# The first FFN layer of the last 512 tokens as seven block products, and a new order of steps

## The chip, the cores and the metric

The kernel runs on one NeuronCore of a Trainium2 chip. The core has engines that each work through a queue of their own in order: TensorE (PE, matrix products, with its weight loads shown apart as PEld), VectorE (DVE), ScalarE (ACT), GpSimd (POOL) and SyncE (SP, which only issues transfers). They wait for one another through semaphores. Products are written to PSUM, which PE, DVE and ACT reach and POOL does not; everything else lies in SBUF. The metric is the device time of one execution in microseconds (us).

## The reference

Windowed attention over 4 sequences of 768 tokens, 8 heads of 64, followed by a feed-forward network on all 3072 tokens with 512 features. A query sees the first 8 keys and the last 96 keys up to its own, with a bias that falls with distance.

```python
scores = scale * np.matmul(q, k.transpose(0, 1, 3, 2)) + bias     # per batch and head
scores = np.where(keep, scores, -1e9)                             # 8 global keys, 96 local ones
a = softmax(scores)
x = np.matmul(a, v).transpose(0, 2, 1, 3).reshape(3072, 512)
h = x @ w_in                                                      # 512 -> 2048
g = np.maximum(h, 0.0) + np.log1p(np.exp(-np.abs(h)))             # softplus
out = g @ w_out                                                   # 2048 -> 512, float32
```

## The kernel before

The 3072 tokens are 24 blocks of 128 for attention (index n, six to a sequence) and 12 chunks of 256 for the feed-forward network (index c, so chunk c takes blocks 2c and 2c+1). Everything is issued by one list of step names, `ORDER` (L564 on), written out in the file: the loop at its end calls one small function for each name, and each engine's queue gets its instructions in that order. Nothing is reordered later. The pools of tiles decide which step has to wait for which buffer.

The steps that matter here, with their names in the list:

- `lq`, `lk`, `lv`, `wi`, `wo`: loads, issued by POOL, which also turns float32 to 16 bits on the way (L101, L107, L112).
- `t`, `d`, `qc`, `kc`, `s`, `ss`, `ab`, `ac`, `e`, `p`, `nm`: transposes, scores, bias, exponential, product with v and normalisation of an attention block. `gk`, `gv` (L254, L259) copy the 8 global rows of k and v into the neighbouring block's tile.
- `x`, `xc`, `y`: the attention output transposed into `XT[c]`, bf16, 512 features by 256 tokens.
- `f` (`ffn1`, L410): the first layer, 8 steps a chunk, each two blocks of 128 hidden features: 8 matmuls of 256 columns into one bank `hT`, of which there are two.
- `fe`, `fl` (`soft`, `plus`): exponential by ACT out of `hT`, then ln(1 + x) by ACT into `G[c]`, float16.
- `o`, `os`: the second layer of chunk 0 in the plain way.
- `m` (`prod`, L499), `ev` (`evict`, L524), `pr` (`pair`, L549), `gs` (`g_sum`, L474), `wd`: the second layer of chunks 1 to 11 as seven block products after Strassen and Winograd: sums of blocks of G by DVE, differences of w_out blocks made once, each product evicted by DVE, two of the sums by POOL.
- `st`: stores, issued by SP. `g` (`gate`, L559): a one-element copy on POOL that makes the loads behind it wait for a step of ACT.

The functions of these steps follow; the seven products of `m` are listed as `BLOCKS`, and `ffn1` in the same place has the plain product.

Of the kernel before, what the change touches and what calls it, by code (L numbers as in the profile page):

```python
# [20 lines left out]
def kernel(  # L21
# [279 lines left out]
    def sc(n, half):  # L301

        if n < NPB:
            buf = early(n, half)
            qk(n, half, lambda r: buf[:, r, :], pre=True)
            return
        qk(n, half, lambda r: s_ps[:, r, :])

# [8 lines left out]
    def add_bias(n, half):  # L317

        Z = new_Z(n, half)
        if n == first_of(n):  # L320
            nc.vector.tensor_tensor(Z[:, 0:4, :], s_ps[:, 0:8:2, :], bias0[:, half, :, :], ALU.add)
        else:
            nc.vector.tensor_tensor(Z[:], s_ps[:], biasA[:, half, :, :], ALU.add)  # L323

    def add_bias2(n, i):

# [9 lines left out]
    def ex(n, half):  # L336
        nreg = 4 if n == first_of(n) else 8
        Pb = work4.tile([P, 8, P], BF16, tag="Pb", name="Pb")
        if n < NPB:
# [86 lines left out]
    def plus(c, u):  # L426
        if c not in G:
            G[c] = ffn.tile([P, NFB, CT], F16, tag="G", name="G")
        nc.scalar.activation(  # L429
            G[c][:, 2 * u : 2 * u + 2, :], ES.pop((c, u))[:], AF.Ln, bias=1.0  # L430
        )

    def o_bank(i):
# [125 lines left out]
    def gate(s):  # L559
# [3 lines left out]

    ORDER = """  # L564
        w18 bb1.0 cq0 ck0 bb0.0 lq1 tq0 lk1 tk0 lv0 z0.0 lk2 z0.1 s0.0 bb0.1 e0.0 lq2 bb1.1 t1 qc1.0
        kc1.0 lv1 s0.1 e0.1 lk3 lq3 z1.0 s1.0 e1.0 p0.0 nm0.0 z1.1 s1.1 t2 qc2.0 kc2.0 lv2 lv3 z2.0
        wi0 e1.1 wi1 p0.1 nm0.1 gk2 p1.0 nm1.0 p1.1 nm1.1 gv2 s2.0 z2.1 wi2 lq4 e2.0 s2.1 e2.1 t3
        qc3.0 kc3.0 gk3 x0 xc0.1 z3.0 p2.0 nm2.0 p2.1 nm2.1 s3.0 x1 xc1.0 e3.0 z3.1 lk4 gv3 s3.1 x2
        xc2.0 e3.1 p3.0 nm3.0 f0 fe0 fl0 lq5 p3.1 nm3.1 f1 fe1 fl1 wi3 x3 xc3.0 f2 fe2 f10 fe10 fl2
        gk4 gv4 fl10 t4 f9 fe9 qc4.0 f8 kc4.0 s4.0 f11 lk5 ab4.0 fe8 t5 qc5.0 fl9 fl8 wi4 fe11 fl11  # L570
        kc5.0 s4.1 ab4.1 e4.0 f3 fe3 fl3 f4 fe4 e4.1 gk5 s5.0 lv4 p4.0 fl4 ab5.0 f5 f12 s5.1 nm4.0
        p4.1 gv5 fe12 e5.0 fe5 fl5 fl12 wo0 o0 f13 nm4.1 x4 wi6 fe13 fl13 o4 f15 fe15 f14 lv5 wo1
        ab5.1 e5.1 p5.0 nm5.0 f6 wd1.0 wd1.1 fe6 p5.1 fl6 nm5.1 xc4.0 o1 o5 wo2 x5 xc5.0 gs1.3 fl15
        wo3 lq6 g11 fe14 fl14 g15 f7 wd3.0 fe7 o6 o2 f17 lk6 fl7 o7 f21 t6 gs1.1 gs1.2 fe21 qc6.1
# [24 lines left out]
        m5.5.0 ev5.5 nm16.0 fl54 ss17 ab17.0 ac17.1 fe51 fl51 d18 ac17.0 f52 p16.1 nm16.1 pr4.1 g47
        fe52 f59 g39 m4.3.0 gk18 lk19 g43 f56 ss18 lq19 fl52 lv17 fe59 e17.0 gv17 fe56 p17.0 e17.1  # L600
        ev4.3 nm17.0 g41 f58 lq20 lk20 ab18.0 f57 fl56 p17.1 fl59 ac18.1 fe58 fe57 fl57 gs6.3 nm17.1
        lv18 st3.1 e18.0 m5.2.0 st3.0 ac18.0 m6.1.1 f61 p18.0 ev5.2 f62 fe62 gs6.1 m6.5.0 gs6.2
        gs5.4 d19 fl58 ev6.1 fe61 fl61 ev6.5 ss19 gk20 ab19.0 f63 m7.1.0 e18.1 f60 fe63 ac19.1 y16
        lv20 ev7.1 nm18.0 ac19.0 y17 m6.6.1 p18.1 d20 pr5.0 m5.4.0 ev6.6 nm18.1 m5.3.1 g57 gs7.3
        ev5.3 e19.0 lv19 p19.0 nm19.0 f69 fl62 fe60 f64 e19.1 lk21 fl60 fl63 gs7.1 p19.1 gs7.2 gk19
        fe69 fl69 y18 ss20 f65 nm19.1 lq21 d21 y19 ev5.4 ab20.0 gk21 fe64 fe65 fl64 gv20 e20.0 f70
        m6.7.0 fe70 ac20.1 fl65 f71 fe71 lk22 p20.0 m7.5.1 ac20.0 e20.1 lq22 d22 fl71 f66 fe66 ev6.7
        pr5.1 ev7.5 pr6.0 m7.6.0 gs6.4 nm20.0 ss21 ab21.0 ev7.6 fl66 p20.1 f68 fe68 lv21 f67 fl68
        e21.0 ac21.1 gv21 nm20.1 m6.2.0 ac21.0 m6.4.1 fe67 e21.1 g53 p21.0 lk23 lq23 st4.1 g51 fl70
        f72 st4.0 ev6.4 ev6.2 g61 f75 nm21.0 g55 lv22 y20 pr7.0 p21.1 pr6.1 fe72 gk22 ss22 nm21.1  # L610
        fl67 ab22.0 m7.7.0 gv22 ev7.7 ac22.1 ac22.0 g49 g67 fl72 fe75 e22.0 f74 f77 m6.3.0 g65
        m8.1.1 d23 y21 p22.0 st5.1 fe77 fl75 e22.1 fl77 fe74 gv12 fl74 ev6.3 gk23 lv23 gs7.4 ev8.1
        f78 m7.2.0 nm22.0 gs8.1 p22.1 g59 st5.0 ev7.2 gv23 ss23 ab23.0 ac23.1 ac23.0 fe78 fl78 f76
        fe76 f73 e23.0 g63 fe73 m7.4.0 m8.5.1 fl73 nm22.1 p23.0 e23.1 f80 fe80 fl76 f85 nm23.0 p23.1
        fe85 fl85 ev7.4 ev8.5 gs9.3 pr7.1 m9.1.0 y22 st6.0 gs8.2 ev9.1 f87 f79 fl80 fe87 m7.3.1
        nm23.1 fe79 fl79 fl87 gs9.1 ev7.3 f84 fe84 f83 m8.6.0 m9.5.1 gs9.2 ev8.6 fl84 gs8.4 fe83 f82
        m8.2.0 st6.1 fe82 fl82 f86 fe86 fl86 f81 ev8.2 g69 fe81 fl81 gs8.3 pr8.0 m8.7.0 ev9.5 ev8.7
        y23 st7.0 m9.2.1 fl83 f93 m9.6.0 st7.1 ev9.2 f88 ev9.6 m8.4.1 ev8.4 m8.3.0 ev8.3 pr8.1 gv19
        fe88 fe93 fl93 fl88 f90 g73 fe90 m10.1.1 ev10.1 f95 fe95 fl90 fl95 gv18 f91 m9.7.0 f89
        gs10.1 gs10.2 gs10.4 m10.6.1 ev10.6 pr9.0 fe91 gs10.3 ev9.7 fe89 f92 f94 m10.7.1 gs9.4 fl91  # L620
        fl89 ev10.7 gs11.3 m10.5.0 fe94 ev10.5 st8.0 st8.1 m10.4.1 ev10.4 pr10.1 fl94 fe92 st10.1
        fl92 gs11.1 m9.4.0 ev9.4 pr9.1 m9.3.1 ev9.3 gs11.2 st9.0 st9.1 m11.1.0 ev11.1 m11.5.1 ev11.5
        m11.6.0 ev11.6 pr10.0 m11.7.1 ev11.7 m11.4.0 ev11.4 pr11.1 m10.2.1 pr11.0 st11.1 ev10.2
        gs11.4 m10.3.0 ev10.3 m11.2.1 st10.0 m11.3.2.1 ev11.2 ev11.3.1 st11.0.1 m11.3.2.0 ev11.3.0
        gv13 st11.0.0
    """

    def warm(count):
# [74 lines left out]
```

## Time and profile before

| | |
|---|---|
| median of 3 runs | 208.21 us (206.58 to 208.42) |
| the profiled execution | 207.14 us, span 205.3 us from the first to the last instruction |
| PE busy | 198.9 us, 97% of the span |
| ACT busy | 154.8 us, 75% |
| DVE busy | 151.0 us, 74% |
| POOL busy | 94.2 us, 46% |
| granted TensorE clock | 0.998 of full speed |

Busy times are of the profiled execution. A row of the timeline gives the start, the time until the group's end, engine, line, operation, the tiles written and read, and the count; square brackets hold the idle time before it and what ended that. A row of a group gives busy time and the mean of one, then the idle time before. A row of the stretches gives the busy time of each engine in a part of the span, with the number of instructions in parentheses.

### The profile page before, as it was taken

How to read it: one execution, taken by the hardware profiler on the slowest of the kernel's cores; microseconds unless marked ns; L12 is line 12 of the kernel's file. 1: busy time of each engine (PE TensorE's matmuls, PEld its weight loads, DVE VectorE, ACT ScalarE, POOL GpSimd, SP SyncE). 2: the span in 40 equal slices, each digit the busy share in tenths (PEclk: the TensorE clock that was granted, in tenths of full speed). 3: DMA queues.
4: the chain of work that ended last, by engine and by line, in shares of the span. 5: the costliest groups of instructions: out<-in, count | busy, mean ns of one | idle time of the engine just before them, and what ended most of it. 6: DMA issues, size and time to landing. Idle time of an engine off the chain costs nothing.

```text
span 205.3 us, 5684 instructions
## 1 busy us (share of the span) xinstructions
PE 198.9 (97%) x2247; PEld 166.3 (81%) x2249; DVE 151.0 (74%) x364; ACT 154.8 (75%) x254; POOL 94.2 (46%) x141
## 2 busy tenths in 40 slices
PE   7999999999999999999999999999999999999992
PEld 2567877677888889898898889889888998888881
DVE  7575464998999996798847889797888855245751
ACT  3977999846699897897987886979899895577300
POOL 8999720388366624539578014781331002200420
PEclk9999999999999999999999999999999999999999
DMA  8999999999999999999999966999457242020132
GB/s 127 150 163 175 190 200 203 158 128 113 167 135 130 109 226 123 147 144 116 209 148 149 160 147 72 125 120 155 128 88 147 28 128 105 0 102 5 65 140 104
DMA packets 109899, 26.85 MB, mean 131 GB/s; under 512 B 101680, under 2 KB 106928, under 8 KB 109872
## 3 DMA queue, kind: packets, MB, share of 16 engines
q0 software_dynamic: 78080, 13.37, 90.1%
q1 hardware_dynamic: 30752, 12.85, 33.5%
q8 instruction: 17, 0.28, 0.6%
q10 hardware_dynamic: 1040, 0.26, 0.6%
q14 instruction: 10, 0.08, 0.1%
HBM read 27.26 MB, written 6.29 MB: 163 GB/s over the span
## 4 chain that ended last, share of the span: by engine, by line
PE 83%; POOL 7%; DMA 4%; issue 2%; DVE 1%; ACT 1%; POOLq 0%
PE hT L416 37%; PE o L510 32%; PE x_ps L359 5%; DMA w_in<-in_moe_w_in_dram 4%; PE s_ps L268 3%; PE o L442 3%; POOL q_t L101 2%; POOL k_t L101 2%; PE s_lo L268 2%; POOL v_t L101 1%; POOL w_in L107 1%; ACT e_sb L424 1%; POOL v_t L259 1%; PE tr L395 0%; PE o_end L510 0%
## 5 line engine op out<-in xcount | busy, mean ns | idle before, releaser
L416 PE MATMUL hT<-XT,w_in 128*128 128x256 bf16 x768 | 95.7, 273 | 0.5 <-DVE rcp L374 0.3
L416 PEld LDWEIGHTS <-w_in 128*128 128x128 bf16 x768 | 72.1, 98 | 11.3 <-DMA w_in<-in_moe_w_in_dram 1.0
L424 ACT ACTIVATE e_sb<-hT 128x512 f32<-128x512 f32 x96 | 56.1, 589 | 26.3 <-PE hT L416 24.9
L429 ACT ACTIVATE G<-e_sb 128x512 f16<-128x512 f32 x96 | 58.0, 624 | 1.8
L343 ACT ACTIVATE Pb<-Z 128x1024 bf16<-128x1024 f32 (+1 forms) x40 | 39.1, 982 | 3.6 <-DVE Z L323 2.1
L510 PEld LDWEIGHTS <-sum 128*128 128x128 f16 x360 | 33.8, 98 | 4.0
L510 PE MATMUL o<-w_dif,sum 128*128 128x256 f16 x264 | 32.9, 273 | 0.0
L510 PEld LDWEIGHTS <-G 128*128 128x128 f16 x264 | 25.6, 98 | 2.9
L101 POOL DMA_DIRECT2D v_t<-in_v_dram x24 | 21.6, 903 | 11.1 <-PE hT L416 10.3
L323 DVE TENSOR_TENSOR Z<-s_ps,biasA 128x1024 f32<-128x1024 f32 x19 | 23.1, 1217 | 2.8 <-PE s_ps L268 2.2
L510 PE MATMUL o<-w_out,G 128*128 128x256 f16 x176 | 22.6, 273 | 0.0
L555 POOL TENSOR_TENSOR osb<-u,p 128x256 f32<-128x256 f32 x11 | 9.0, 826 | 29.1 <-DVE p L543 11.6
L101 POOL DMA_DIRECT2D q_t<-in_q_dram x23 | 20.9, 911 | 2.4 <-DMA w_in<-in_moe_w_in_dram 1.8
L562 POOL CAST gate_t<-G 1x1 bf16<-1x1 f16 x32 | 6.8, 211 | 32.9 <-ACT G L429 32.4
L101 POOL DMA_DIRECT2D k_t<-in_k_dram x23 | 20.6, 897 | 1.9 <-PE x_ps L359 0.7
L553 POOL TENSOR_TENSOR d<-b,p 128x256 f32<-128x256 f32 x11 | 8.4, 768 | 25.9 <-DVE b L539 23.6
L377 DVE TENSOR_TENSOR xsf<-x_ps,rcp 128x256 bf16<-128x256 f32 x44 | 18.7, 425 | 1.5
L359 PEld LDWEIGHTS <-Pb 128*128 128x128 bf16 x352 | 16.0, 97 | 2.6 <-issue 0.5
L359 PE MATMUL x_ps<-v_t,Pb 128*128 128x65 bf16 x324 | 17.1, 193 | 0.4 <-ACT G L429 0.4
L483 DVE TENSOR_TENSOR sum<-G 128x1024 f16<-128x1024 f16 x22 | 15.2, 693 | 2.1 <-ACT G L429 2.1
L268 PEld LDWEIGHTS <-KT 64*128 64x128 bf16 x352 | 9.9, 94 | 6.1 <-issue 4.4
L374 DVE RECIPROCAL rcp<-x_ps 128x4 f32<-128x4 f32 x44 | 7.7, 175 | 7.8 <-PE x_ps L359 7.5
(87 smaller groups left out, 213.8 us busy)
## 6 DMA issues: line engine op xcount, KB each, us to landing
out_dram<-osb SPq DMA_DIRECT2D x23, 256.0 KB, 2.8
v_t<-in_v_dram POOLq DMA_DIRECT2D x24, 128.0 KB, 5.5
q_t<-in_q_dram POOLq DMA_DIRECT2D x23, 128.0 KB, 5.1
k_t<-in_k_dram POOLq DMA_DIRECT2D x23, 128.0 KB, 5.2
w_out<-in_moe_w_out_dram POOLq DMA_DIRECT2D x4, 512.0 KB, 14.4
w_in<-in_moe_w_in_dram POOLq DMA_DIRECT2D x4, 256.0 KB, 7.0
w_in<-in_moe_w_in_dram POOLq DMA_DIRECT2D x2, 512.0 KB, 10.4
k_f<-in_k_dram ACTq DMA_DIRECT2D x1, 256.0 KB, 4.4
```

What stands on the lines that cost most here:

```text
L101: nc.gpsimd.dma_start(dst[n][:, :, 0:D], src[b, :, i * P : (i + 1) * P, :].rearrange("h s d -> s h d"))
L268: nc.tensor.matmul(dst(4 * sub + 2 * mm + t), KT[n - t][rows, m, :], QT[n][rows, m, :], start=not pre, stop=not pre or (mm == 1 and (t == ...
L323: nc.vector.tensor_tensor(Z[:], s_ps[:], biasA[:, half, :, :], ALU.add)
L343: nc.scalar.activation(Pb[:, 0:nreg, :], src, AF.Exp, scale=inv_sqrt)
L359: nc.tensor.matmul(x_b[:, lh, :], Pb[:, r, :], v_t[n - t][:, h, :], start=(t == 0), stop=(t == 1 or first),)
L377: nc.vector.tensor_tensor(xsf[:, h0 : h0 + 4, :], x_b[:, :, 0:D], rcp[:, h0 : h0 + 4][:, :, None].to_broadcast([P, 4, D]), ALU.mult,)
L416: nc.tensor.matmul(hT[:, j, :], w[:, m, fo : fo + P], XT[c][:, m, :], start=(m == 0), stop=(m == KM - 1),)
L424: nc.scalar.activation(ES[c, u][:], HT.pop((c, u))[:], AF.Exp)
L429: nc.scalar.activation(G[c][:, 2 * u : 2 * u + 2, :], ES.pop((c, u))[:], AF.Ln, bias=1.0)
L483: nc.vector.tensor_tensor(SM[c, i][:], a(), b(), op)
L510: nc.tensor.matmul(o[:, 0 : c1 - c0], lhs[:, k, :], rhs(k)[:, c0:c1], start=(k == 0), stop=(k == NU - 1),)
L555: add(OSB[c, 1][:, CT : 2 * CT], OSB[c, "u"][:], OSB[c, "p5"][:], ALU.add)
```

## The change

The first layer of chunks 10 and 11 (tokens 2560 to 3071) is no longer made by `f`, `fe` and `fl`. Its 512 x 2048 weight and the 512 x 256 token chunk are cut into two halves each way, and the four block results are made from seven block products, in two halves of the hidden features (index u):

- `hw` (`w_sum_part`): four sums and differences of weight blocks, for each u, float16, made by POOL; eight steps in all, one or two instructions each.
- `ht` (`x_dif`): four differences of token blocks for a chunk, by DVE.
- `h` (`h_prod`): one of the seven products, 8 matmuls of 128 columns (four blocks of features, two steps of contraction) into an `hT` bank.
- `hv` (`h_sum`): takes the bank out: products 1 and 5 as copies by ACT, the other five as additions by DVE to what is there.
- `hp` (`h_pair`): two further additions of 512 columns by POOL.
- `he`, `hl`: exponential in place in SBUF and ln(1 + x) into `G[c]`, by ACT, for each of four block results and each u.

All steps behind the first loads stand in a new order. `z`, `sc`, `add_bias` and `ex` are rewritten so that a block without a bias product could be planned; the new list has the bias product for all of the first four blocks, as before. Loads keep their number and sizes.

```diff
+    def w_sum_part(i, u):
+        op = nc.gpsimd.tensor_tensor
+        t = {n: w_sum[n, u] for n in (1, 2, 3, 4)}
+        if i == 1:
+            for (a, at), (b, _) in zip(w_quarter(1, 0, u), w_quarter(1, 1, u)):
+                op(t[1][:, :, at], a, b, ALU.add)
+        elif i == 2:
+            for a, at in w_quarter(0, 0, u):
+                op(t[2][:, :, at], t[1][:, :, at], a, ALU.subtract)
...
+    def x_dif(c, i):
+        HD[c, i] = sums.tile([P, KH, P], F16, tag=f"x_dif{i}", name=f"x_dif{i}", bufs=1)
...
+        nc.vector.tensor_tensor(HD[c, i][:], a, b, ALU.subtract)
...
+    def h_prod(c, i, u):
+        hT = ps2.tile([P, HB, P], F32, tag="hT", name="hT")
...
+        for b in range(HB):
+            for k in range(KH):
+                nc.tensor.matmul(hT[:, b, :], lhs(k, b), rhs[:, k, :], start=(k == 0), stop=(k == KH - 1))
...
+    def h_sum(c, i, u):
+        o = HT.pop((c, i, u))[:]
...
+        if i == 1:
+            nc.scalar.copy(HS[c, "s", u][:], o)
+        elif i == 5:
+            nc.scalar.copy(HS[c, "p", u][:], o)
+        elif i in (2, 4):
+            nc.vector.tensor_tensor(HS[c, i, u][:], t["s" if i == 2 else "u"][:], o, ALU.add)
+        elif i == 7:
+            nc.vector.tensor_tensor(HS[c, "u", u][:], t["s"][:], o, ALU.add)
+        else:
+            nc.vector.tensor_tensor(t["s"][:], t["s"][:], o, ALU.add)
+    def h_pair(c, which, u):
+        t = HS[c, "s" if which == 0 else "u", u]
+        nc.gpsimd.tensor_tensor(t[:], t[:], HS[c, "p", u][:], ALU.add)
+    def h_exp(c, q, u):
+        t = h_of(c, q, u)
+        nc.scalar.activation(t[:], t[:], AF.Exp)
+    def h_plus(c, q, u):
...
+        nc.scalar.activation(G[c][:, b0 : b0 + HB, P * j : P * j + P], h_of(c, q, u)[:], AF.Ln, bias=1.0)
```

The new list around the places that the prediction names:

```
kc1.0 lv1 s0.1 e0.1 z1.0 lq3 lk3 lv2 p0.0 nm0.0 s1.0 p0.1 nm0.1 z1.1 s1.1 t2 e1.0 x0 qc2.0
kc2.0 z2.0 wi1 p1.0 e1.1 gk2 nm1.0 wi0 p1.1 s2.0 xc0.1 e2.0 z2.1 s2.1 t3 nm1.1 qc3.0 x1
kc3.0 e2.1 gk3 gv2 p2.0 lv3 xc1.0 z3.0 p2.1 z3.1 nm2.0 nm2.1 s3.0 e3.0 s3.1 gk4 e3.1 f1 fe1
f0 wi2 fl1 wi3 gv3 p3.0 x2 nm3.0 xc2.0 p3.1 nm3.1 lk4 fe0 fl0 f2 fe2 gv4 x3 xc3.0 f3 lq4 fl2
...
pr1.0 lv9 p9.0 m2.6.1 nm9.0 d10 f27 gk10 ev2.5 p9.1 hw3.0 lv10 lk12 fl30 ev2.6 d11 ss10 g29
...
nm17.1 ac18.0 e18.1 fe56 hw1.0 m4.3.0 f60 ev4.3 fl56 gs6.4 d19 pr4.1 ss19 fe60 y16 p18.0
ab19.0 ac19.1 m6.6.0 nm18.0 f57 ev6.6 fl60 f62 m5.2.1 fe57 y17 p18.1 m5.4.0 g47 st3.0 nm18.1
lv19 st3.1 ev5.2 ev5.4 fl57 f61 e19.0 p19.0 m6.5.1 lk20 ac19.0 gs6.3 d20 fe62 fe61 fl62
...
ab21.0 e21.0 g51 g49 lq22 lk23 f68 fe68 fl67 ev6.7 nm20.0 lv21 ac21.0 ac21.1 f71 fe71 m5.3.0
...
nm22.0 fe78 g57 ss23 f76 e22.1 ab23.0 ac23.1 ac23.0 f73 fl77 fl78 fe76 fe73 m8.5.0 y21 st5.0
ht10.3 st5.1 fl76 pr6.1 ht10.1 h10.1.0 ht10.2 p22.1 hv10.1.0 hw2.1 lv23 nm22.1 g63 h10.2.0
gv23 hv10.2.0 e23.0 e23.1 m7.2.1 h10.1.1 hv10.1.1 p23.0 hw2.0 ev7.2 h10.6.0 nm23.0 m7.4.1
hv10.6.0 ev8.5 p23.1 nm23.1 g61 h10.5.0 pr7.0 h10.7.0 ht10.4 m7.3.0 fl73 ev7.4 hv10.5.0
he10.11.0 hv10.7.0 ev7.3 hl10.11.0 h10.4.0 hv10.4.0 he10.21.0 y22 h10.2.1 hv10.2.1 hw4.0
m8.1.1 h10.6.1 hw3.1 gs9.1 st6.1 he10.11.1 hl10.11.1 h10.5.1 hv10.5.1 m9.1.0 hv10.6.1 y23
gs8.4 ev8.1 h10.7.1 ev9.1 hw4.1 hv10.7.1 g65 hp10.0.0 hp10.1.0 he10.22.0 gs9.2 h10.4.1
m8.6.1 ev8.6 h10.3.0 hl10.21.0 hv10.3.0 m8.7.0 hv10.4.1 ev8.7 gs9.3 ht11.3 m8.2.1 h10.3.1
...
hv11.3.1 h11.4.1 he11.12.0 he11.22.0 hl11.22.0 hv11.4.1 hp11.1.1 he11.12.1 hl11.12.0
```

More of the change, by code (lines that the diff above doesn't have):

```diff
@@ L278, in early @@
         return (oo if half else s_ps)[:, :, :]
+    BIASED = set()
     def z(n, half):
+        BIASED.add((n, half))
         buf = early(n, half)
@@ L319, in add_bias @@
         Z = new_Z(n, half)
+        buf = early(n, half) if n < NPB else s_ps
         if n == first_of(n):
[L321 removed]
+            nc.vector.tensor_tensor(Z[:, 0:4, :], buf[:, 0:8:2, :], bias0[:, half, :, :], ALU.add)
         else:
[L323 removed]
+            nc.vector.tensor_tensor(Z[:], buf[:, 0:8, :], biasA[:, half, :, :], ALU.add)
     def add_bias2(n, i):
@@ L430, in plus, with w_quarter @@
             G[c][:, 2 * u : 2 * u + 2, :], ES.pop((c, u))[:], AF.Ln, bias=1.0
+        )
+    HB = NFB // 4
+    KH = KM // 2
+    w_sum = {
+        (i, u): const.tile([P, KH, HB * P], F16, name=f"w_sum{i}_{u}") for i in (1, 2, 3, 4) for u in (0, 1)
+    }
+    def w_quarter(i, j, u):
+        first = 8 * i + HB * u
+        out, fb = [], first
+        while fb < first + HB:
+            w, fo = w_in_of(fb)
+            n = min(w.shape[2] - fo, (first + HB - fb) * P)
+            out.append((w[:, KH * j : KH * j + KH, fo : fo + n], slice((fb - first) * P, (fb - first) * P + n)))
+            fb += n // P
+        return out
@@ new lines, in h_lhs, with lhs @@
+    def h_lhs(i, u):
+        quarter = {1: (0, 0), 2: (0, 1), 4: (1, 1)}.get(i)
+        if quarter is None:
+            t = w_sum[{3: 4, 5: 1, 6: 2, 7: 3}[i], u]
+            return lambda k, b: t[:, k, b * P : b * P + P]
+        parts = w_quarter(*quarter, u)
+        def lhs(k, b):
+            for w, at in parts:
+                if at.start <= b * P < at.stop:
+                    return w[:, k, b * P - at.start : b * P - at.start + P]
+        return lhs
+    def h_prod(c, i, u):
+        hT = ps2.tile([P, HB, P], F32, tag="hT", name="hT")
+        lhs = h_lhs(i, u)
+        rhs = {
+            1: lambda: x_block(c, 0, 0), 2: lambda: x_block(c, 1, 0), 3: lambda: x_block(c, 1, 1),
+        }.get(i, lambda: HD[c, {4: 4, 5: 1, 6: 2, 7: 3}[i]][:])()
+        for b in range(HB):
+            for k in range(KH):
+                nc.tensor.matmul(hT[:, b, :], lhs(k, b), rhs[:, k, :], start=(k == 0), stop=(k == KH - 1))
+        HT[c, i, u] = hT
@@ L604 @@
[L604 to L614, printed above, removed]
@@ L662 @@
         "wd": w_dif_part, "gs": g_sum, "m": prod, "ev": evict, "pr": pair, "st": store, "xc": copy_x,
+        "ht": x_dif, "hw": w_sum_part, "h": h_prod, "hv": h_sum, "hp": h_pair, "he": h_exp, "hl": h_plus,
     }
```

134 lines of the change are left out of this document (83 added, 51 removed).

## The prediction

> **What bounds the kernel now.** I read the busy table and the chain that ended last first, to see which engine sets the end, and then the timeline of TensorE (PE), to see whether its stream has holes.
>
> ```profile
> span 205.3 us, 5684 instructions
> PE 198.9 (97%) x2247; PEld 166.3 (81%) x2249; DVE 151.0 (74%) x364; ACT 154.8 (75%) x254; POOL 94.2 (46%) x141
> ...
> PE 83%; POOL 7%; DMA 4%; issue 2%; DVE 1%; ACT 1%; POOLq 0%
> ...
> L416 PE MATMUL hT<-XT,w_in 128*128 128x256 bf16 x768 | 95.7, 273 | 0.5 <-DVE rcp L374 0.3
> ```
>
> PE is busy 97% of the span and is 83% of the chain; the rest of the chain is the loading at the start. The busy time of a matmul row includes a pipelined tail (273 ns mean), so the price of a matmul is the distance between starts. It is read where one group follows another:
>
> ```profile
> 180.23 1.04 PE L510 MATMUL o<-w_out,sum 128*128 128x256 f16 x8
> 181.10 1.04 PE L416 MATMUL hT<-XT,w_in 128*128 128x256 bf16 x8
> 181.97 1.04 PE L510 MATMUL o<-w_out,G 128*128 128x256 f16 x8
> ```
>
> Eight matmuls of 256 columns take 0.87 us, 109 ns each, and the next group starts at once. So in the late part PE has no holes: what the change saves on PE there is saved in full, unless another engine becomes late. The stretches tell where others are nearly full:
>
> ```profile
> 30.00:70.00 40.00, 39.65 (x453) 31.48 (x452) 34.20 (x76) 31.20 (x51) 22.50 (x32) 1.00 1.83 145
> 152.00:184.00 32.00, 32.00 (x329) 28.69 (x327) 19.45 (x43) 23.88 (x41) 4.96 (x10) 1.00 0.37 85
> 184.00:201.00 17.00, 17.00 (x164) 15.30 (x163) 11.03 (x25) 6.08 (x11) 3.96 (x5) 1.00 0.17 64
> ```
>
> The columns are length, then busy time (and count) of PE, weight loads, DVE, ACT, POOL, then granted clock (1.00, full), DMA share, GB/s. From 30 to 70 us DVE is busy 34.2 of 40 us and PE still loses only 0.35 us: a DVE at 86% has not yet stopped PE. From 152 to 201 us DVE has 30.5 us of work in 49, POOL 8.9. That is the room into which the change puts its additions.
>
> **The change part by part.** *Matmuls.* The first layer of chunks 10 and 11 loses 2 x 64 matmuls of 256 columns and gains 2 x 7 x 16 = 224 of 128 columns (seven products, two halves, four blocks, two contraction steps). Removed: 128 x 109 ns = 13.95 us. The price of 128 columns, each with its own weights, is read from the transposes and from the last product:
>
> ```profile
> 12.73 0.40 PE L211 MATMUL tr<-ident,q_t 128*128 128x128 bf16 x4
> 12.97 0.39 PE L211 MATMUL tr<-ident,k_t 128*128 128x128 bf16 x4
> 13.19 0.39 PE L395 MATMUL tr_x<-ident,xsf 128*128 128x128 bf16 x4
> ...
> 200.31 1.06 PE L510 MATMUL o_end<-w_out,sum 128*128 128x96 f16 x16
> ...
> 35.21 0.41 PE L359 MATMUL x_ps<-v_t,Pb 128*128 128x65 bf16 x8
> 35.46 1.03 PE L416 MATMUL hT<-XT,w_in 128*128 128x256 bf16 x8
> ```
>
> Four transposes take 0.22 to 0.24 us, 55 to 60 ns each. The last row holds eight matmuls of 160 and eight of 96 columns, 128 on average, in 1.06 us less the same 0.17 us tail (1.04 - 0.87): 56 ns each. Added: 224 x 56 ns = 12.54 us. **PE term: -1.4 us**, all on the path.
>
> Could the weight loads forbid that price? Their rows show 98 ns each:
>
> ```profile
> L416 PEld LDWEIGHTS <-w_in 128*128 128x128 bf16 x768 | 72.1, 98 | 11.3 <-DMA w_in<-in_moe_w_in_dram 1.0
> ```
>
> Were that the spacing, 224 x 98 = 21.95 us, +8.0 us instead of -1.4. The L359 rows above speak against it: eight 65-column matmuls, each with a full load, start and finish their turn in 0.25 us, 31 ns each, so loads overlap one another and stand below 56 ns. The Trainium skill, page "TensorE: Matmul & The Clock Gate", section "Back-to-back issue gap", gives about 81 ns as the sustained spacing of 128-column matmuls in a stream of load and matmul pairs. By that estimate the new products would take 18.1 us, and the term would be +4.2 us; the rows of this trace do not agree with it.
>
> *Vector and scalar work.* Prices:
>
> ```profile
> 46.11 0.68 DVE L483 TENSOR_TENSOR sum<-G,sum 128x1024 f16<-128x1024 f16 x1
> 46.71 0.68 DVE L321 TENSOR_TENSOR Z<-s_ps,bias 128x512 f32<-128x512 f32 x1
> 47.31 0.41 DVE L332 TENSOR_TENSOR Z<-s_lo,bias 128x256 f32<-128x256 f32 x1
> 47.64 0.42 DVE L332 TENSOR_TENSOR Z<-o,bias 128x256 f32<-128x256 f32 x1
> ...
> L424 ACT ACTIVATE e_sb<-hT 128x512 f32<-128x512 f32 x96 | 56.1, 589 | 26.3 <-PE hT L416 24.9
> L429 ACT ACTIVATE G<-e_sb 128x512 f16<-128x512 f32 x96 | 58.0, 624 | 1.8
> ...
> L377 DVE TENSOR_TENSOR xsf<-x_ps,rcp 128x256 bf16<-128x256 f32 x44 | 18.7, 425 | 1.5
> ...
> L374 DVE RECIPROCAL rcp<-x_ps 128x4 f32<-128x4 f32 x44 | 7.7, 175 | 7.8 <-PE x_ps L359 7.5
> ```
>
> Back to back, DVE starts a new instruction 0.60 us after one of 512 f32 or 1024 f16 columns, and 0.33 us after one of 256 f32, 0.08 less than the duration. `h_sum` adds 20 additions of 512 columns out of PSUM (as L321): 12.0 us by steps, 13.6 by durations. The 8 token differences (`x_dif`, 256 f16 columns) have no row; a quarter of L483 and a whole 256-column row bound them at 0.17 and 0.42 us, and I take 0.2 a step, nearer to the f16 row: 1.6 us. ACT gains 8 copies of the L424 kind, 4.7 us; the 16 exponentials and 16 logarithms stay, the exponentials reading SBUF (624 against 589 ns: +0.6 us).
>
> Where do they stand? In the new list the 28 products lie between `h10.1.0` and `h11.4.1`, with 16 block products of the second layer and 3 groups of attention: 28 x 0.45 + 16 x 0.87 + 3 x 0.25 = 27.2 us of PE. DVE has there 20 additions (12.0), 6 differences (1.2), 16 evictions (16 x 0.33 = 5.3), 8 sums of G (4.8), three normalisations (0.6 each by the two rows below) and a copy: 25.3 us, 93%. By durations it is 29.6 us, more than PE has. PE cannot run ahead: a product fills an `hT` bank in 0.45 us, there are two banks, and the bank's eviction takes 0.6 us behind whatever DVE has in hand; behind DVE wait the evictions of the second layer, and behind those PE. Bounds of this term: 0 (the steps fit, as at 30 to 70 us) and 29.6 - 27.2 = +2.4 us. I take **+0.7 us**, nearer to the steps.
>
> *GpSimd.* An addition of 256 columns and a one-element copy give its price:
>
> ```profile
> L555 POOL TENSOR_TENSOR osb<-u,p x11: 717/755/1210, 66.5 to 197.6; 128x256 f32<-128x256 f32 x11
> ...
> L101 POOL DMA_DIRECT2D v_t<-in_v_dram x24 | 21.6, 903 | 11.1 <-PE hT L416 10.3
> ...
> L562 POOL CAST gate_t<-G 1x1 bf16<-1x1 f16 x32 | 6.8, 211 | 32.9 <-ACT G L429 32.4
> ...
> v_t<-in_v_dram POOLq DMA_DIRECT2D x24, 128.0 KB, 5.5
> ```
>
> With about 0.2 us fixed (the gate), 2.2 ns a column: 512 columns 1.3 us, 1024 columns 2.5 us. Bounds for a w_in piece: 0.76 (as for 256 columns) and 4 x 0.76. The eight `w_sum_part` steps are 12 pieces of 512 and 2 of 1024, 21 us; the eight `h_pair` steps 10.7 us. On POOL (46% busy) that is room enough, but three of the parts stand ahead of loads: `hw3.0` ahead of `lv10` and `lk12`, `hw1.0` ahead of `lv19`, `hw2.1` ahead of `lv23`. From `hw2.1` to `p23.0`, which uses `lv23`, the list has only 1.8 us of PE between, and part, issue and landing need 2.7 + 0.9 + 5.5 = 9.1 us. It is hidden only because POOL waits for nothing late: the last thing before it is the pair `pr6.1`, whose inputs are complete (`ev6.7`) 20 us of PE work earlier. If that cover is gone the price is up to 7 us. For `hw3.0` and `hw1.0` the same sum leaves some microseconds. The parts also finish ahead of their products, `hw4.1` last, about when `h10.1.0` starts. What I do charge is the neighbour:
>
> ```profile
> 66.45 1.21 POOL L555 TENSOR_TENSOR osb<-u,p 128x256 f32<-128x256 f32 x1
> 67.00 0.70 DVE L254 COPY KT<-KT 128x32 bf16<-128x32 bf16 x1
> 133.89 0.73 POOL L553 TENSOR_TENSOR d<-b,p 128x256 f32<-128x256 f32 x1 [1.84 <-DVE b L539]
> 134.28 0.89 DVE L483 TENSOR_TENSOR sum<-G 128x1024 f16<-128x1024 f16 x1
> L254 DVE COPY KT<-KT x14: 165/170/801, 19.7 to 155.6; 128x32 bf16<-128x32 bf16 x14
> ```
>
> A KT copy that takes 0.17 us took 0.70 until POOL's addition ended at 67.66; a G sum that takes 0.68 took 0.89 beside one. A DVE instruction behind a POOL addition can so wait out its rest, and the additions are now 1.3 to 2.5 us instead of 0.76. Two or three such hits in the middle, of 0.7 us each with DVE at 86%, I price at **+0.3 us** (bounds 0 and 2.5).
>
> *The start.* All steps behind the first loads are ordered anew. The first product waits for a weight load:
>
> ```profile
> 11.78 0.61 POOL L259 COPY v_t<-v_t 8x520 bf16<-8x520 bf16 x1
> 12.35 0.75 POOL L107 DMA_DIRECT2D w_in<-in_moe_w_in_dram  x1
> ...
> 16.79 0.77 PEld L416 LDWEIGHTS <-w_in 128*128 128x128 bf16 x8 [0.43 <-DMA w_in<-in_moe_w_in_dram]
> ...
> 19.39 1.64 PEld L416 LDWEIGHTS <-w_in 128*128 128x128 bf16 x16 [0.25 <-DMA w_in<-in_moe_w_in_dram]
> ...
> DMA to landing us min/median/max: 6.4/7.0/12.1
> ```
>
> The third `w_in` part, issued at 12.35, was waited for at 19.39: 7.0 us. The new list issues the first part (now `wi1`) one load earlier, -0.9 us, by putting `lv3` behind the copy `gv2`. That copy waits for attention products and ran at 11.78; if it does so again, `lv3` is issued at 12.4 and `wi2` at 13.3, +0.9 us, while `wi3` comes three loads earlier. The bytes up to the fifth part are the same. I expect up to 1 us gained or lost and take **+0.2**. Whether the 0.35 us of PE that the old order lost between 30 and 70 us are lost again I leave at 0. The last products, evictions and stores are as before: 0.
>
> **Sum:** -1.4 + 0.7 + 0.3 + 0.2 = -0.2 us on the span, 205.1. The profiled execution took 207.14 us, 1.84 outside the span; so 206.9 for its like. It lies 1.07 below the median of 208.21, and the four times shown (206.58, 207.14, 208.21, 208.42) average 207.59. I predict 207.59 - 0.2 = 207.4. About 1% (2.1 us) is what a measurement of this kernel can tell from no change.
>
> **The rivals.**
> 1. *The PE saving arrives whole.* DVE keeps up as it did from 30 to 70 us and the start gains 0.9: -1.4 - 0.9 = -2.3, 205.3 us. For: the late PE stream has no hole at all today. Against: DVE's 93%. Chance 0.17.
> 2. *POOL's additions hold DVE back until DVE sets the pace late (slower).* In the last 45 us POOL gets six parts and eight pairs, 26 us, busy 60% of the time; some 20 DVE instructions there (sums of G, differences, short copies) are of the kind that waited above. Each would lose 0.6 x 0.67 = 0.4 us, 8 us in all if they spread evenly. It decides once the loss exceeds DVE's free 2 us. At half the hits the term is 4 - 2 = 2 us beyond mine, at all of them 6; with 3: 210.4 us. For: the 0.70 and 0.89 us rows. Against: the parts run early and bunched. The Trainium skill, page "SBUF — State Buffer", section "Who interferes with whom", states that the side that starts second blocks until the first is finished when a vector instruction has two SBUF inputs or uses its two-port mode; by that rule this rival is more likely than the two rows alone make it, and the trace agrees with it (0.70 against 0.17 us). Chance 0.22.
> 3. *Weight loads set the spacing of the short matmuls*, at the middle between 56 and 98 ns: 224 x 21 ns = +4.7 us, 212.1. The 31 ns spacing speaks against it; Chance 0.03. The 81 ns of the Trainium skill (page cited above) would be this case.
> 4. *The sums are not made in advance*: POOL is later than I think, and `lv23` or a product waits for it. +3 us, 210.4; chance 0.05.
>
> **How the numbers follow.** The forecast, -1.4 to +1.8 about 207.6, has 0.53. The range reaches into rival 1 below (205.3) and through most of 2 and 4 above: 205.2 to 211.0. Faster by over 1%: half of rival 1 and the lower edge of the forecast as times scatter, 0.19. Slower by over 1%: rivals 2 to 4 less their mild ends, 0.25. Within: 0.56. The likeliest case's own range is 206.2 to 209.4.
>
> **What would show it.** Right: `h_prod` groups of eight starting 0.45 us apart; PE without idle rows before the first `h_prod`; the DVE row near 90% from 155 to 185 us, with short PE holes that DVE evictions end. Rival 2: KT copies, differences and sums of G lengthened to 1 us and more beside `w_sum`, and PE waiting for `h_sum` or `evict`. Rival 4: weight loads of `h_prod` or attention that wait for POOL or a v load. I am wrong if PE's total falls by clearly more or less than 1.4 us, or if the difference lies ahead of 150 us.

## The result, and the profile after

The changed kernel takes 218.3 us (median of six runs, 217.43 to 219.56) beside 206.67 us for the kernel before (median of six, 206.01 to 208.42): a ratio of 1.055, 95% interval 1.049 to 1.061. Forecast were 207.4 us and a range up to 211.0. The profiled execution has a span of 216.5 us against 205.3. These are the page's total, its busy row and its chain by engine, and then the three stretches of the prediction, with the same columns (length, busy time and count of PE, weight loads, DVE, ACT, POOL, then clock, DMA share, GB/s):

```profile
span 216.5 us, 5951 instructions
PE 201.5 (93%) x2345; PEld 167.3 (77%) x2345; DVE 177.9 (82%) x392; ACT 159.4 (74%) x262; POOL 124.0 (57%) x163
PE 64%; DVE 20%; DMA 6%; issue 4%; POOL 3%; DVEq 0%; POOLq 0%
```

```profile
30.00:70.00 40.00, 39.82 (x463) 31.60 (x462) 35.16 (x78) 32.38 (x53) 22.32 (x32) 1.00 1.86 142
152.00:184.00 32.00, 29.88 (x384) 26.88 (x382) 29.97 (x62) 22.56 (x38) 16.14 (x16) 1.00 0.29 63
184.00:201.00 17.00, 14.84 (x182) 13.10 (x180) 16.59 (x28) 10.72 (x19) 7.67 (x9) 1.00 0.17 64
```

PE's share of the chain fell from 83% to 64%; DVE's rose from 1% to 20%. Up to 70 us PE is as full as before. From 152 to 201 us, where it had no hole, it now stands still for 4.3 of 49 us, and DVE is busy for 46.6. But most of the loss is not there. The timeline of the changed kernel has two large holes ahead of 150 us (start, duration, engine and line, tiles; in brackets the idle time before it and what ended it):

```profile
113.51 2.48 DVE L259 COPY v_t<-v_t 8x520 bf16<-8x520 bf16 x1
113.69 2.14 POOL L463 TENSOR_TENSOR w_sum<-w_in 128x1024 f16<-128x1024 bf16 x1
115.92 0.40 DVE L667 TENSOR_TENSOR b<-a,o 128x256 f32<-128x256 f32 x1
116.37 1.03 PE L638 MATMUL o<-w_dif,sum 128*128 128x256 f16 x8 [1.10 <-DVE b L667]
...
142.33 2.23 DVE L254 COPY KT<-KT 128x32 bf16<-128x32 bf16 x1
142.41 2.11 POOL L463 TENSOR_TENSOR w_sum<-w_in 128x1024 f16<-128x1024 bf16 x1
144.62 0.28 PE L268 MATMUL s_ps<-QT,KT 64*128 64x128 bf16 x4 [1.04 <-DVE KT L254]
147.40 2.96 PE L420 MATMUL hT<-XT,w_in 128*128 128x256 bf16 x13
```

In each a short copy on DVE (a KT copy alone takes 0.17 us in the prediction's L254 row) stands for over 2 us beside a weight sum and ends with it (113.69 + 2.14 = 115.83, the copy at 115.99; 144.52, the copy at 144.56). Both copies begin a little ahead of the weight sum (113.51 against 113.69, 142.33 against 142.41), while GpSimd is still busy with what stands before it, the issue of a load and a one-element copy. DVE takes its instructions in order, so the eviction at 115.92 is late, and PE behind it. The last row shows a second price: 13 matmuls started at 147.40 take 2.96 us; at 109 ns each they would take 1.4 us and the tail. The clock in that stretch, with the same columns as above:

```profile
147.00:150.50 3.50, 3.50 (x25) 2.63 (x23) 2.45 (x6) 3.38 (x6) 2.68 (x3) 0.51 0.37 68
```

PE was granted 0.51 of its clock; over 3.5 us that is about 1.7 us of lost work, an estimate from this row. In the last stage the same picture has GpSimd's paired additions as the neighbour, a G sum as the held operation, and a block product of PE behind it:

```profile
176.60 1.28 POOL L543 TENSOR_TENSOR hu<-hu,hp 128x512 f32<-128x512 f32 x1
176.93 1.50 DVE L611 TENSOR_TENSOR sum<-G 128x1024 f16<-128x1024 f16 x1
179.09 0.61 PE L515 MATMUL hT<-x_dif,w_sum 128*128 128x128 f16 x8 [0.36 <-DVE hs L538]
```

A G sum takes 0.68 us alone; here 1.50. So the theory to be tested is: **(1)** GpSimd's new additions hold back those operations of DVE that work in SBUF alone (16-bit copies and sums here) until they end, and PE waits for DVE. The rivals: **(2)** DVE simply has too much work from its 20 new additions, wherever GpSimd stands; **(3)** the new order of the steps loses the time.

### The profile page after: what moved, and what is told of

It reads as the page before. It is cut to its first block, busy times and chain, and to the rows that moved or that the text cites. A ratio compares the mean times of both kernels' runs of the same rounds, so it can differ in the third digit from the quotient of the medians.

```text
span 216.5 us, 5951 instructions
## 1 busy us (share of the span) xinstructions
PE 201.5 (93%) x2345; PEld 167.3 (77%) x2345; DVE 177.9 (82%) x392; ACT 159.4 (74%) x262; POOL 124.0 (57%) x163
## 4 chain that ended last, share of the span: by engine, by line
PE 64%; DVE 20%; DMA 6%; issue 4%; POOL 3%; DVEq 0%; POOLq 0%
PE hT L420 28%; PE o L638 21%; PE x_ps L363 4%; DMA w_in<-in_moe_w_in_dram 4%; PE o L570 3%; DVE sum L611 3%; PE s_ps L268 3%; DMA v_t<-in_v_dram 2%; DVE Z L327 2%; DVE hs L538 2%; DVE v_t L259 2%; PE hT L515 2%; DVE KT L254 2%; DVE x_dif L490 1%; DVE e_sb L533 1%
## 5 line engine op out<-in xcount | busy, mean ns | idle before, releaser
L420 PE MATMUL hT<-XT,w_in 128*128 128x256 bf16 x640 | 80.8, 276 | 0.4 <-ACT G L433 0.4
L420 PEld LDWEIGHTS <-w_in 128*128 128x128 bf16 x640 | 61.1, 99 | 9.9 <-DMA w_in<-in_moe_w_in_dram 0.7
L428 ACT ACTIVATE e_sb<-hT 128x512 f32<-128x512 f32 x80 | 46.8, 590 | 16.0 <-PE hT L420 15.5
L433 ACT ACTIVATE G<-e_sb 128x512 f16<-128x512 f32 x80 | 48.3, 624 | 1.1
L638 PE MATMUL o<-w_dif,sum 128*128 128x256 f16 x264 | 33.7, 273 | 1.4 <-DVE b L667 1.1
L638 PEld LDWEIGHTS <-G 128*128 128x128 f16 x264 | 25.0, 98 | 2.8
L690 POOL CAST gate_t<-G 1x1 bf16<-1x1 f16 x32 | 7.5, 235 | 28.7 <-ACT G L433 28.2
L681 POOL TENSOR_TENSOR d<-b,p 128x256 f32<-128x256 f32 x11 | 9.3, 844 | 21.1 <-DVE b L667 9.0
L611 DVE TENSOR_TENSOR sum<-G 128x1024 f16<-128x1024 f16 x22 | 17.0, 772 | 0.8 <-ACT G L557 0.4
L683 POOL TENSOR_TENSOR osb<-u,p 128x256 f32<-128x256 f32 x11 | 8.5, 781 | 14.1 <-DMA out_dram<-osb 7.8
```

The costliest lines, as they stand in the source:

```text
L420: nc.tensor.matmul(hT[:, j, :], w[:, m, fo : fo + P], XT[c][:, m, :], start=(m == 0), stop=(m == KM - 1),)
L428: nc.scalar.activation(ES[c, u][:], HT.pop((c, u))[:], AF.Exp)
L433: nc.scalar.activation(G[c][:, 2 * u : 2 * u + 2, :], ES.pop((c, u))[:], AF.Ln, bias=1.0)
L611: nc.vector.tensor_tensor(SM[c, i][:], a(), b(), op)
L638: nc.tensor.matmul(o[:, 0 : c1 - c0], lhs[:, k, :], rhs(k)[:, c0:c1], start=(k == 0), stop=(k == NU - 1),)
L681: add(part_sum(c, "d"), OSB[c, "b"][:], OSB[c, "p5"][:], ALU.add)
```

## The experiments

**Each kind of GpSimd addition taken away.** First the weight sums, cut to one column:

```diff
-        op = nc.gpsimd.tensor_tensor
+        def op(o, a, b, kind):
+            nc.gpsimd.tensor_tensor(o[:, :, 0:1], a[:, :, 0:1], b[:, :, 0:1], kind)
...
-        quarter = {1: (0, 0), 2: (0, 1), 4: (1, 1)}.get(i)
+        quarter = {1: (0, 0), 2: (0, 1), 4: (1, 1)}.get(i, (1, 0))
```

> The changed kernel with GpSimd's weight sums cut to one column each; the products that used them read a block of w_in instead, so the weight sums are left out of what is computed. Matrix products, DVE's additions, the paired additions and the order are those of the changed kernel. Theory 1 (GpSimd's additions hold DVE's fast copies and sums back until they end, and PE waits for those): the holes of PE at 115.0 (1.26 us), 143 to 150 (2.3 us, and about 1.6 us of matmuls at the lower clock behind them), 153.5 (0.7) and 164.5 (1.4) go, together 7.2 us: 210 to 212.5 us against 218.3. Theory 2 (DVE has too much work from its 20 new additions, wherever GpSimd stands): within 1.5 us of 218.3. Theory 3 (the new order of the steps loses the time): within 1.5 us of 218.3.

Measured: 209.91 us, ratio to the kernel before 1.016 (1.012 to 1.020). That is 8.4 us less than 218.3, a little more than theory 1 gave and far from what 2 and 3 gave. Between 110 and 150 us PE has no idle time left (length, PE, weight loads, DVE and so on as above):

```profile
110.00:150.00 40.00, 40.00 (x485) 35.03 (x484) 32.90 (x76) 34.31 (x55) 20.37 (x39) 1.00 1.53 147
```

Where the 8.4 us lie is told by the first block product, in the changed kernel and, below, without the weight sums:

```profile
169.00 0.61 PE L515 MATMUL hT<-XT,w_in 128*128 128x128 bf16 x8
```

```profile
160.33 0.61 PE L517 MATMUL hT<-XT,w_in 128*128 128x128 bf16 x8
```

The first product comes 8.67 us earlier, and the spans differ by 8.7 us (216.5 and 207.8). From the first product to the last both take 30.33 us (to 199.33 and 190.66). So all that the weight sums cost in these two profiles lies ahead of the block products; some 0.8 us of the 8.67 are there by 24 us, before the first weight sum starts at 56.70, and are not theirs. GpSimd had ended all eight weight sums by 168.06 us.

Then the paired additions alone, and both:

```diff
-        nc.gpsimd.tensor_tensor(t[:], t[:], HS[c, "p", u][:], ALU.add)
+        nc.gpsimd.tensor_tensor(t[:, :, 0:1], t[:, :, 0:1], HS[c, "p", u][:, :, 0:1], ALU.add)
```

> The changed kernel with GpSimd's eight paired additions cut to one column of each 128, so three quarters of two quadrants lack one product; all else as in the changed kernel. Theory 1: of the holes behind 175 us those beside these additions go, 2 to 3.5 us: 214.5 to 216.5 us. Theories 2 and 3: 217 to 219 us.

> Both of GpSimd's kinds of additions of the changed kernel cut to one column (the weight sums and three quarters of two quadrants' paired additions are left out); PE's block products, DVE's 20 additions and the order stay. Theory 1 (GpSimd's additions are the loss): the two savings add up, 8.4 and 2.9 us of 218.3: 206 to 208.5 us, and below the order alone (208.0) by at most PE's 1.4 us. Theory 2 (DVE's own new additions cost time in the last stage too): 209 us or more, with PE holes behind DVE sums that no GpSimd addition touches.

Measured: 215.42 us without the pairs (1.042, 1.038 to 1.047), so they cost 2.9 us; these do lie in the last stage, where the products take 27.58 us from first to last instead of 30.33. Without both it is 206.53 us (1.000, 0.997 to 1.003). The sum of the two savings, 11.3, gives 207.0; together they are 11.8. A late stretch of the run without both:

```profile
152.00:184.00 32.00, 31.61 (x425) 28.87 (x424) 30.75 (x65) 25.14 (x44) 7.94 (x19) 1.00 0.20 53
```

DVE is busy 30.75 of 32 us, 96%, with all its new additions, and PE loses 0.4 us there (and 0.2 from 184 to 201 us). Theory 2 falls as the explanation of the 11.6 us by which the changed kernel is slower.

Without these additions GpSimd's loads also start earlier, so loads that come late would be cured as well. The changed kernel's profile speaks against that: from 60 to 205 us no wait that the list of waits shows for PE or for its weight loads ends on a load or on GpSimd; beside PE's own issue it names DVE alone.

In the run without the pairs the weight sums still hold, now at another place, and the clock falls again after the hole:

```profile
149.64 3.11 DVE L259 COPY v_t<-v_t 8x520 bf16<-8x520 bf16 x1
150.34 2.26 POOL L466 TENSOR_TENSOR w_sum<-w_sum,w_in 128x512 f16<-128x512 f16 x2
152.80 0.37 PE L363 MATMUL x_ps<-v_t,Pb 128*128 128x65 bf16 x7 [2.07 <-DVE v_t L259]
```

```profile
154.00:157.50 3.50, 3.50 (x26) 2.63 (x24) 2.35 (x7) 2.45 (x4) 0.00 (x0) 0.52 0.08 17
```

**The order alone.** The changed kernel's list, with tokens 2560 to 3071 as 16 whole first-layer steps; the start of the late part:

```diff
-h10.4.0 hv10.4.0 he10.21.0 y22 h10.2.1 hv10.2.1 hw4.0 m8.1.1 h10.6.1 hw3.1
+f80 fe80 fl80 y22 f81 fe81 fl81 m8.1.1 f82 fe82 fl82
```

> The changed kernel's order with tokens 2560 to 3071 taken as whole products as before (16 ffn1 steps with their exp and ln put where the late block products stood; no weight sums, no differences, no additions). It computes the same function. Theory 3 (the new order loses the time): over 213 us. Theories 1 and 2: 206.5 to 210 us, of which 1 to 1.5 us is the start.

Measured: 208.0 us, 1.0066 (1.0038 to 1.0094). Theory 3 falls: the order costs 1.4 us of the 11.6. The profiled spans of the order alone and of the run without GpSimd's additions are 205.9 and 204.3 us. These two differ in the block products, DVE's additions and ScalarE's copies, and not in GpSimd's work: 1.6 us of span, 1.5 us of the medians, for the block products.

**The disputed cost by itself.** The weight sums put into the kernel before, at places where GpSimd was idle, and read by nobody:

```diff
-lv18
+lv18 hw3.0 hw1.0
...
-lv22
+lv22 hw1.1 hw2.1
...
-g49
+g49 hw2.0
...
-g69
+g69 hw4.0 hw3.1 hw4.1
```

> The kernel before with the eight steps of weight sums on GpSimd added at places where GpSimd was idle, their results not used. It measures the disputed cost alone: no step of PE, DVE or ScalarE is added or moved. Theory 1: each of the ten additions holds DVE's fast copies and G sums that meet it, 2 to 6 us: 208.5 to 213 us, with copies of global tokens and G sums of 1 to 2.5 us beside the additions. Theories 2 and 3: 206 to 208 us, as before.

Measured: 210.15, 219.18, 219.54 and 221.09 us, beside 206.58. No interval is given: one execution is 3.6 us above the kernel before at full clock, and three are 12.6 to 14.5 us above it at a mean clock of 0.97 to 0.98. What can be set against the kernel before is the 3.6 us, from one execution of which there is no profile. The profile is of a long one (219.54 us), so it gives no price; it shows what can happen when a copy meets a whole run of additions:

```profile
162.72 2.25 POOL L466 TENSOR_TENSOR w_sum<-w_in,w_sum 128x512 f16<-128x512 bf16 x2
162.82 6.74 DVE L259 COPY v_t<-v_t 8x520 bf16<-8x520 bf16 x1
164.95 2.25 POOL L463 TENSOR_TENSOR w_sum<-w_in,w_in 128x512 f16<-128x512 bf16 x2
167.16 2.25 POOL L466 TENSOR_TENSOR w_sum<-w_in,w_sum 128x512 f16<-128x512 bf16 x2
171.34 1.87 PE L545 MATMUL o<-w_dif,sum 128*128 128x256 f16 x8 [5.62 <-DVE Z L332]
```

```profile
172.00:176.00 4.00, 4.00 (x32) 3.15 (x31) 2.71 (x7) 2.49 (x5) 0.00 (x0) 0.62 0.50 54
```

Six additions stand back to back from 162.72 to 169.41, and the copy goes from 162.82 to 169.56. It is not let in between two of them. PE then waits for the bias addition behind the copy, 5.62 us, and runs on at 0.62 of its clock. No step of PE, DVE or ScalarE was added or moved, and all four waits of PE over 0.15 us behind the start (0.43, 2.36, 0.23 and 5.62 us) end on DVE. I had expected at most 213 us, which the one short execution keeps and the three long ones do not: the run of additions as one hold was not in that number.

**The copies taken out of the way.** First in the changed kernel, from group 17 on:

```diff
-            copy_by(n < NPB)(KT[n - 1][:, :, 0:NG], KT[first_of(n)][:, :, 0:NG])
+            copy_by(n < NPB or n > 16)(KT[n - 1][:, :, 0:NG], KT[first_of(n)][:, :, 0:NG])
...
-            copy = (nc.gpsimd if n < NPB else nc.vector).tensor_copy
+            copy = nc.gpsimd.tensor_copy if n < NPB else copy_by(n > 16)
```

> The changed kernel with the copies of the global tokens' keys and values (groups of eight lines, groups 17 to 23) given from DVE to ScalarE; it computes the same. Of the held operations this takes away the copies that stood in PE's way at 115, 143 to 150 and 153.5 us; G sums and differences stay on DVE. Theory 1 with the copies as the victims: 5 to 7 us less, 211 to 213.5 us. Theory 1 with a victim wherever the next fast operation of DVE stands (a G sum is met instead): 214 to 217 us. Theory 2: 217 us or more, since DVE loses hardly any work.

Measured: 213.11, 211.00 and 212.49 us, and one of 214.36 that the ratio of 1.026 (1.019 to 1.033) leaves out. The median of the three, 212.5, is 5.8 us less than 218.3, as the copies as victims gave. The hole at 115 us stayed, against what I wrote: its copy is one of group 16, which the edit left on DVE.

```profile
111.95 0.94 POOL L101 DMA_DIRECT2D v_t<-in_v_dram  x1
112.03 3.17 DVE L259 COPY v_t<-v_t 8x520 bf16<-8x520 bf16 x1
112.91 2.13 POOL L463 TENSOR_TENSOR w_sum<-w_in 128x1024 f16<-128x1024 bf16 x1
115.58 1.03 PE L638 MATMUL o<-w_dif,sum 128*128 128x256 f16 x8 [1.79 <-DVE b L667]
```

This copy began 0.9 us ahead of the addition, while GpSimd issued a load, and was not through when the addition came.

The same edit, from group 15 on, in the kernel before with the added weight sums:

> The kernel before with the same added weight sums on GpSimd as in x3 (results not used), and the copies of the global tokens' keys and values of groups 15 to 23 on ScalarE instead of DVE. In x3 the copies of groups 16 to 23 were held for up to 6.74 us and each long hole of PE stood behind one. If the held copies are the loss of x3: 206.5 to 209 us, with G sums the only held operations left. If the additions cost in another way (GpSimd's own lateness, its loads behind the additions, traffic): as x3, 210 us or more.

Measured: 211.83 us, 1.022 (1.018 to 1.026). By its number that is the second reading, and my expectation for the copies was missed. The timeline says what became of the hold:

```profile
110.71 5.53 DVE L518 TENSOR_TENSOR sum<-sum,G 128x1024 f16<-128x1024 f16 x1
111.33 2.29 POOL L463 TENSOR_TENSOR w_sum<-w_in,w_in 128x512 f16<-128x512 bf16 x2
113.55 2.12 POOL L456 TENSOR_TENSOR w_sum<-w_in 128x1024 f16<-128x1024 bf16 x1
116.62 2.74 PE L545 MATMUL o<-w_dif,sum 128*128 128x256 f16 x12 [2.80 <-DVE a L570]
```

With the copies gone, a G sum met the run of additions and took 5.53 us instead of 0.68; it had begun while GpSimd issued a load. PE waited 2.80 us for the eviction behind it and was granted 0.51 of its clock from 116.5 to 120 us: 2.8 us and, by the clock, about 1.7 make the 4.5 us that this run is slower than its kernel before (207.33). So the cause that the second reading gave, GpSimd's own lateness, is not needed for it, and copies are not the only victims: here the hold fell on the next SBUF operation that DVE had. It is the reading "a victim wherever the next fast operation stands", which I had written down for the run before and not for this one.

**The same sums on DVE.** With the additions on DVE (and their steps moved in the list), the total work of DVE grows and the hold by the weight sums goes:

```diff
-        op = nc.gpsimd.tensor_tensor
+        op = nc.vector.tensor_tensor
```

> The changed kernel with the eight steps of weight sums on DVE, placed between 74 and 130 us, where DVE has 1 to 2 us free of each 10; GpSimd keeps the paired additions. It computes the same. DVE takes an addition of 128x1024 16-bit elements in 0.67 us, so some 5.5 us are added to it. Theory 1: the gain of leaving the sums out stays nearly whole, 209.5 to 211.5 us. Theory 2 (DVE's work is what costs): as slow as the changed kernel or slower, 217 to 221 us.

> The weight sums on DVE again (4.7 us of work as measured in x7), now between about 100 and 150 us, each behind a copy of the global tokens' values instead of ahead of one; the paired additions stay on GpSimd. It computes the same. If x7 lost time because its sums stood ahead of copies that PE waited for, in a stretch where DVE was 97 to 99% busy: 209.5 to 211.5 us, near the run without weight sums (209.9). If DVE's amount of work is what costs: as x7, 213 us or more.

> As x8, and the eight paired additions go to DVE as well, in the last stage, where DVE was 95% busy with held operations and would be about 95% busy with the additions themselves. GpSimd adds nothing that the kernel before had not. It computes the same. Theory 1: the holds of the last stage go (2.9 us), DVE gets 8 additions of at most 0.68 us, 5.4 us, into a stage that it then nearly sets: 207.5 to 210.5 us, under x8. Theory 2 (DVE's amount of work): over x8 by 2 us or more.

Measured: 213.91 us with the sums early (1.034, 1.028 to 1.040), which neither theory had given; 209.86 with the sums later (1.015, 1.011 to 1.019), as without weight sums at all (209.91); 212.23 with the pairs on DVE too (1.028, 1.023 to 1.032). In the early version the sums ran earlier than I had meant (57 to 94 us), where DVE is full (9.90 of 10 us), and ahead of a copy that PE needs:

```profile
70.00:80.00 10.00, 8.99 (x105) 7.20 (x100) 9.90 (x22) 8.64 (x14) 3.20 (x6) 1.00 1.13 145
```

```profile
79.48 1.02 DVE L466 TENSOR_TENSOR w_sum<-w_sum,w_in 128x512 f16<-128x512 f16 x2
80.42 0.43 DVE L259 COPY v_t<-v_t 8x520 bf16<-8x520 bf16 x1
80.91 0.37 PE L363 MATMUL x_ps<-v_t,Pb 128*128 128x65 bf16 x7 [1.63 <-DVE v_t L259]
```

So the same work costs nothing or 4 us by its place on DVE; in the profiles about 1.3 us of that is there by 24 us, before the first of these sums at 57 us, and is not explained by them. With the pairs on DVE in the last stage theory 2 is right in that stage: 2.4 us slower than with GpSimd's holds. None of these versions is below the kernel before; even without GpSimd's additions the change only equals it.

## Why the prediction was wrong

The mechanism that decided was named, as rival 2, with a chance of 0.22; the forecast and the range were wrong because of its size and place.

- **The step that failed: GpSimd's neighbour, +0.3 us (bounds 0 and 2.5).** It measured 11.8 us (218.3 to 206.53). "Two or three such hits in the middle, of 0.7 us each with DVE at 86%" was wrong in number, size and discount. In the changed kernel's profile 11 operations of DVE beside the new additions take 0.3 to 2.2 us longer than their shortest like. A hit can be what is left of GpSimd's whole run, load issues included (3.17, 5.53 and 6.74 us above). DVE's free 14% is no cover: a copy held for 2.48 us stands ahead of an eviction with a PE product behind it, whatever DVE's average. And a lower clock follows some of the holes (13 matmuls in 2.96 us), a price that the sum did not have. "The parts run early and bunched" stood against rival 2; the weight sums did all their harm ahead of the block products, and a bunch is no shelter (6.74 us behind six).
- **Rival 2, 210.4 us, "late", up to 6 us.** Half right: the paired additions in the last stage cost 2.9 us, close to the 2 to 6 us given. But the weight sums cost 8.4 us, most of it ahead of the last 45 us, of which the rival spoke; and the run without them has no PE idle time from 110 to 150 us. The rule that the prediction cited for it, the Trainium skill, page "SBUF — State Buffer", section "Who interferes with whom", says that the side that starts second blocks until the first is finished. These traces agree on "until finished" (2.48 us for a copy beside a 2.14 us addition), and the sum did not use that size. They do not agree on who starts first: this copy began 0.18 us ahead of the addition.
- **PE term, -1.4 us: right.** The order alone against the run without GpSimd's additions gives -1.6 us of span and -1.5 of the medians, with DVE's part in it. The block products start 0.45 us apart, as forecast:

```profile
189.29 0.61 PE L515 MATMUL hT<-XT,w_in 128*128 128x128 bf16 x8
189.74 0.61 PE L515 MATMUL hT<-x_dif,w_sum 128*128 128x128 f16 x8
```

  Eight in 0.45 us are 56 ns each, so rival 3 is out, and with it the 81 ns of the Trainium skill, page "TensorE: Matmul & The Clock Gate", section "Back-to-back issue gap".
- **DVE late, +0.7 us (0 to 2.4): too high, inside its bounds.** DVE at 96% cost PE about 0.4 us, and 0.2 behind 184 us, when no addition on GpSimd held it. The prices held, 0.68 us for a sum out of PSUM (rows in the last section); a difference alone takes 0.28 us, which is the 0.2 assumed once the 0.08 between step and duration is taken off (187.05 us in the changed kernel).
- **GpSimd's own prices: right as bounds, a little high.** 2.1 us for 1024 columns (the rows at 113.69 and 142.41) and 1.15 us for 512 (the four of L466 between 148.5 and 152.9 us), against 2.5 and 1.3.
- **Rival 4, sums not in advance: not seen.** No wait listed for PE or its weight loads from 60 to 205 us ends on GpSimd or on a load; the block products wait for DVE (`hs` in the row at 179.09).
- **The start and the order, +0.2 us: too low.** The order alone costs 1.4 us (0.8 to 1.9). Where it loses them was not tried one by one.
- **"I am wrong if", among others, "the difference lies ahead of 150 us":** most of it does. By the time of the same step of ScalarE the changed kernel is 7.3 us behind the run without weight sums when that run is at 149.5 us.

The bill: 206.6 + 1.4 (order) - 1.5 (block products and DVE's part of them) + 11.8 (GpSimd's additions) = 218.3.

## What to carry to other kernels

An idle engine is not free room if its instructions hold back those of a busy one: before work is given to GpSimd, look in the profile for a DVE operation in SBUF that lasted several times its usual duration beside a GpSimd instruction, and price a hit at up to the rest of GpSimd's run of instructions, not at the excess seen once. Then ask which engine waits in order behind the operation that can be hit. Two things helped here: to give the short copies to ScalarE (5.8 us), and to give the weight sums to DVE at places where no copy on PE's path stood behind them (8.4 us). The paired additions were better left on GpSimd, because DVE was full in their stage. Leaving gaps between GpSimd's additions was not tried.

## What the runs showed of the hardware that I had not expected

The hold can outlast one instruction: with GpSimd's instructions back to back DVE's copy got in behind the sixth (6.74 us). The page "SBUF — State Buffer" of the Trainium skill, section "Who interferes with whom", speaks of a lock for one whole instruction; these runs show a longer one. But not always. In the changed kernel a G sum that met the first of two additions back to back (163.12 to 165.84) got in ahead of the second, which was lengthened from 1.15 to 1.60 us:

```profile
163.28 1.54 DVE L611 TENSOR_TENSOR sum<-G 128x1024 f16<-128x1024 f16 x1
164.23 1.60 POOL L470 TENSOR_TENSOR w_sum<-w_in,w_in 128x512 f16<-128x512 bf16 x1
```

And the six additions that held the copy for 6.74 us cost PE nothing in the run with the copies on ScalarE (163.28 to 170.00 us there): what they cost depends on what DVE meets in that time. When DVE gets in between two additions and when it does not is open.

Only some of DVE's operations are held. The sums that read one operand from PSUM are not, in the middle of a GpSimd addition too, while the G sum behind them is (changed kernel):

```profile
196.48 1.27 POOL L543 TENSOR_TENSOR hu<-hu,hp 128x512 f32<-128x512 f32 x1 [3.88 <-DVE e_sb L533]
196.89 0.69 DVE L536 TENSOR_TENSOR hu<-hs,hT 128x512 f32<-128x512 f32 x1
197.50 0.68 DVE L538 TENSOR_TENSOR hs<-hs,hT 128x512 f32<-128x512 f32 x1
197.72 1.27 POOL L543 TENSOR_TENSOR hs<-hs,hp 128x512 f32<-128x512 f32 x1
198.09 1.45 DVE L611 TENSOR_TENSOR sum<-G,sum 128x1024 f16<-128x1024 f16 x1
```

It works the other way too, and with 32-bit operands: with all sums on DVE, a GpSimd addition that takes 0.72 us took 2.51, while DVE ran a G sum that had begun at 175.40, a token difference and two f32 additions with both inputs in SBUF, one behind the other; it ended 0.67 us after DVE had gone over to a sum out of PSUM at 177.40, so it too was held over several instructions:

```profile
175.56 2.51 POOL L683 TENSOR_TENSOR osb<-u,p 128x256 f32<-128x256 f32 x1 [17.86 <-DVE u L669]
176.20 0.69 DVE L543 TENSOR_TENSOR hs<-hs,hp 128x512 f32<-128x512 f32 x1
176.80 0.69 DVE L543 TENSOR_TENSOR hu<-hu,hp 128x512 f32<-128x512 f32 x1
177.40 0.68 DVE L538 TENSOR_TENSOR hs<-hs,hT 128x512 f32<-128x512 f32 x1
```

Both agree with the same section of the Trainium skill: a vector instruction with at most one SBUF input does not contend outside the two-port modes, one with two does.

And a hole can cost more than itself: after the wait of 2.07 us shown above PE was granted 0.52 of its clock from 154.0 to 157.5 us, and after that of 5.62 us 0.62 from 172 to 176 us. In the changed kernel waits of 1.04, 0.30 and 0.39 us, 1.73 in all between 143 and 146 us, stand ahead of the stretch at 0.51. Yet after a single wait of 1.79 us (the changed kernel with copies on ScalarE) the clock stayed at 1.00 from 116 to 120 us. So the length of the wait alone does not decide it.

The Trainium skill, page "TensorE: Matmul & The Clock Gate", section "What's actually happening", gives an idle window of about 3.4 us for the fall to half clock. Here 2.07 us of waiting were enough. What decides, these runs do not show.
